# First MoE's last block with five sums of 512 columns at once, and the second product of the block before it behind them

## The chip, the cores and the metric

The kernel runs on one core of one Trainium2 chip. The metric is the device time of one execution in microseconds (us); before the change it was 1115.1 us, the median of three runs (1113.62 to 1118.73).

## What is computed

Three stages follow each other on 1792 tokens (4 batches of 448):

```python
x = attention(q, k, v, g_q, g_k)            # 48 heads of 448 x 64, q and k with an RMS norm
h = x @ moe_w_in                            # first MoE: 1792 x 768 by 768 x 1024
solu = h * softmax(h)
ln = (solu - mean(solu)) / sqrt(var(solu) + 1e-06) * moe_g_ln
x2 = ln @ moe_w_out                         # 1024 x 768
h2 = x2 @ moe2_w_in                         # second MoE: 768 x 2048
out = (h2 - tanh(h2)) @ moe2_w_out          # 2048 x 768
```

The weights arrive as 64-bit numbers and are converted to 32 bits on the chip.

## The kernel before, in words

**Precision.** Each product of the two MoEs is made of three matmuls (`three`, lines 181 to 184): both factors are kept as a high and a low part in fp32r, and high by high, high by low and low by high are added up in PSUM. `split` (lines 186 to 188) makes the parts: ScalarE copies the high one (L187), VectorE subtracts it (L188).

**Blocks.** The first MoE goes over the tokens in four blocks of 384, 384, 384 and 640 tokens; the last is made of a part of 384 and a part of 256, the latter with tiles of its own (`xs+`, `hb+`, `lnT+`) in SBUF space that the attention gives back. A block has these steps: `x_split` loads x from DRAM (`xr`, L496) and splits it into `xs`; `moe_h` computes h (`hps`, TensorE) and copies it to `hb` (L529); `layer_norm` works on `hb` (L545 to L568); `moe_lnT` transposes the result (`lps`, L581) and splits it into `lnT`; `moe_x2` multiplies with `w_out` (`x2ps`) and writes x2 to DRAM (`x2d`, L596).

**Stages.** `stage(b)` holds the work of block b up to its layer norm and the transposes and second product of block b-1. Of the six output chunks d of `moe_x2(b-1)`, the first `XB[b]` stand ahead of `moe_h(b)` and the others behind it. `XB` is 2 for stage 3, the last block's, and 0 for the others. Stages 0 to 2 are interleaved with the attention of batches 1 to 3; stage 3 and stage 4 (block 3's transposes and second product) come when the attention is over.

**moe_h.** The 1024 columns of h are done in four groups of 256. In a group the tokens go in pairs of 128; each pair fills one PSUM bank (pool `ps_m`, three banks) with its six row chunks of the weights one after the other. The stationary operand is 128 tokens of `xs`, the moving one 256 columns of the weights. For block 3 VectorE also takes the maximum of each filled bank (`mx`, L524) before ScalarE copies it.

**Weights.** The converted weights of the first MoE are saved in DRAM in pieces of 512 KB and come back by `Stream.conv` (L174) into a pool `w` of five buffers, in the order of a list of items; an `in` item holds 256 rows by 256 columns, high and low. SP issues these loads in its queue, as it does all others of the stage.

**The second MoE's start.** Ahead of stage 3, `w2.conv(6)` calls for six weight pieces of the second MoE (loads of 512 KB on L115, conversion on POOL, VectorE and ScalarE) and `x2_load(0)` loads and splits x2 of its first 256 tokens (L735, `x2s`). The second MoE's first sums, `h2ps`, take their banks from pool `ps_h`, five banks that the attention held before.

**The order on each engine** is not the order of the code: a planner puts the instructions in the order of its own time model, earlier code first among what is ready in it, and an engine then runs its queue strictly in that order. So work that stands later in the code can come earlier in a queue, where it found a gap.

Of the kernel before, what the change touches and what calls it, by code (L numbers as in the profile page):

```python
# [8 lines left out]
F32 = mybir.dt.float32  # L9
F32R = mybir.dt.float32r  # L10
I32 = mybir.dt.int32
AF = mybir.ActivationFunctionType
ALU = mybir.AluOpType
AX = mybir.AxisListType
# [4 lines left out]
def kernel(  # L19
# [14 lines left out]
    nc = tc.nc  # L34
    B, H, S, D = q.shape
    NTOK, DM = out.shape
    F1 = moe_w_out.shape[0]
# [12 lines left out]
    blocks = [[(0, 384, "")], [(384, 384, "")], [(768, 384, "")], [(1152, 384, ""), (1536, 256, "+")]]  # L50
    NBK = len(blocks)

    XB = [0, 0, 0, 2, 0]

    NQ = 3
    needs = [-(-(b[-1][0] + b[-1][1]) // S) - 1 for b in blocks]
# [25 lines left out]
    def source(kind, i):  # L82
        if kind == "out":
            d, half = divmod(i, 2)
            src = moe_w_out[512 * half:512 * half + 512, 256 * d:256 * d + 256]
            return src.rearrange("(c p) (f z) -> p c f z", p=128, z=2), (4, 128)
        r, c = divmod(i, 3)
        if kind == "out2":
            src = moe2_w_out[256 * r:256 * r + 256, 512 * c:512 * c + 512]
        else:  # L90
            src = (moe_w_in if kind == "in" else moe2_w_in)[256 * c:256 * c + 256, 512 * r:512 * r + 512]
        return src.rearrange("(c p) (f z) -> p c f z", p=128, z=2), (2, 256)

    saved = {}

    class Stream:
# [70 lines left out]
        def conv(self, n):  # L167
            while self.nc < min(n, len(self.items)):
                self.load(self.nc + 1)
                kind, i, again = self.items[self.nc]  # L170
                if again:
                    a, b = source(kind, i)[1]
                    w = self.pool(kind, i).tile([128, 2, a, b], F32R, tag="w6", name="w6")
                    nc.sync.dma_start(out=w.bitcast(F32), in_=saved[kind, i])  # L174
                else:
                    w = self.convert(kind, i, self.pool(kind, i), self.save)
                self.got[self.nc] = self.wide if kind == "out2" else w
                self.nc += 1
                self.load(self.nc + 2)
# [307 lines left out]
    Bp = {}  # L487
    xs_b, hb_t, ln_g, mx_t = {}, {}, {}, {}

    def x_split(b):  # L490
        xs_b[b] = []
        for t0, T, z in blocks[b]:
            xs = Bp["xs" + z].tile([128, 2, KD, T], F32R, tag="xs", name="xs")
            for j in range(0, KD, 2):
                xr = Bp["xr"].tile([128, 2, T], F32, tag="xr", name="xr")
                nc.sync.dma_start(out=xr, in_=xd[:, j:j + 2, t0:t0 + T])  # L496
                split(xs[:, 0, j:j + 2], xs[:, 1, j:j + 2], xr)
            xs_b[b].append(xs)

    def moe_h(b):  # L500
        w0 = w_at["in", b]
        ws.conv(w0 + 3)
        xs_all = xs_b.pop(b)
        hb_t[b] = []
        if b == NBK - 1:
            mx_t[b] = Bp["small"].tile([128, tokens[b] // 128, F1 // 256], F32, tag="mx", name="mx")
        for t0, T, z in blocks[b]:
            hb_t[b].append([Bp["hb" + z].tile([128, F1], F32, tag="hb", name="hb") for _ in range(T // 128)])
        for qq in range(F1 // 256):
            for (t0, T, _), xs, hb in zip(blocks[b], xs_all, hb_t[b]):  # L510
                for tp in range(0, T // 128, 2):
                    n = min(2, T // 128 - tp)
                    ps = ps_m.tile([128, n, 256], F32, tag="m", name="hps")
                    for zi in range(n):
                        cols = slice(128 * (tp + zi), 128 * (tp + zi) + 128)
                        for c in range(KD):
                            w = ws.got[w0 + 3 * qq + c // 2]
                            three(
                                ps[:, zi], (xs[:, 0, c, cols], xs[:, 1, c, cols]),
                                (w[:, 0, c % 2], w[:, 1, c % 2]), c == 0, c == KD - 1,  # L520
                            )
                    if b == NBK - 1:
                        u0 = (t0 - blocks[b][0][0]) // 128 + tp
                        nc.vector.tensor_reduce(  # L524
                            out=mx_t[b][:, u0:u0 + n, qq:qq + 1].rearrange("p u o -> p (u o)"), in_=ps,
                            axis=AX.X, op=ALU.max, negate=True,
                        )
                    for zi in range(n):
                        nc.scalar.activation(  # L529
                            out=hb[tp + zi][:, 256 * qq:256 * qq + 256], in_=ps[:, zi], func=AF.Copy  # L530
                        )
                    if t0 == blocks[b][0][0] and tp == 0:
                        ws.conv(w0 + 3 * qq + 6)
                        if b == 1:
                            for i in range(3 * qq, 3 * qq + 3):
                                ws.convert("out", i, Bp["w"], True)
                    yield n * 1.97

    def layer_norm(b):
        for iu, u in enumerate([u for hb in hb_t[b] for u in hb]):  # L540
# [30 lines left out]
    def moe_lnT(b):  # L571
        ln_g[b] = []
        for (t0, T, y), hb in zip(blocks[b], hb_t.pop(b)):
            G = Bp["lnT" + y].tile([128, 2, KF1, T], F32R, tag="lnT", name="lnT")
            ln_g[b].append(G)
            for t, u in enumerate(hb):
                cols = slice(128 * t, 128 * t + 128)
                for z in range(2):
                    ps = ps_m.tile([128, 4, 128], F32, tag="m", name="lps")
                    for c in range(4):  # L580
                        nc.tensor.transpose(ps[:, c], u[:, 512 * z + 128 * c:512 * z + 128 * c + 128], idf)  # L581
                    split(G[:, 0, 4 * z:4 * z + 4, cols], G[:, 1, 4 * z:4 * z + 4, cols], ps)
                yield 0.9

    def moe_x2(b, d0, d1):
# [13 lines left out]
        if d1 == KD:  # L599
            ln_g.pop(b)  # L600

    def stage(b):

        if b < NBK:
            x_split(b)
        if b > 0:
            yield from moe_lnT(b - 1)
        ln = iter(())
        if b < NBK:
            yield from moe_x2(b - 1, 0, XB[b])  # L610
            yield from moe_h(b)
            ln = layer_norm(b)
            if b == 0:
                for _ in ln:
                    yield 0.5
        if b > 0:
            for cost in moe_x2(b - 1, XB[b], KD):
                next(ln, None)
                yield cost
        for _ in ln:  # L620
            yield 0.5
# [29 lines left out]
    for b in range(NBK + 1):  # L651
        for d in range(KD + 1):
            if d == XB[b] and b < NBK:
                w_at["in", b] = len(items)
                items += [("in", i, b > 0) for i in range(12)]
            if d < KD and b > 0:
                w_at["out", b - 1, d] = len(items)
                items += [("out", i, True) for i in (2 * d, 2 * d + 1)]
# [124 lines left out]
        if sp == NSP - 1 and i < NB - 1:  # L783
            nc.sync.dma_start(out=out[t0:t0 + T, :].rearrange("(t p) d -> p t d", p=128), in_=ob[i])

    w2.conv(6)
    x2_load(0)
    while b <= NBK:
        overlap(b, None)
        b += 1  # L790
# [50 lines left out]
```

## Time and profile before

| | |
|---|---|
| median of three runs | 1115.1 us (1113.62 to 1118.73) |
| profiled execution | 1117.29 us |
| its span, first to last instruction | 1115.4 us |
| TensorE matmuls busy | 1045.5 us, 94% of the span |
| VectorE, ScalarE, POOL busy | 694.8, 493.8 and 234.2 us |
| mean granted TensorE clock | 0.987 of full speed |

The attention ends at about 510 us, stages 3 and 4 lie between 510 and 645 us, the second MoE's main part behind them. A matmul's busy time in the rows is longer than its share of the pipeline: matmuls overlap, and the distance from one start to the next is what TensorE needs for one.

### The profile page before, as it was taken

What the parts mean: (1) busy time and instruction counts of PE and PEld (TensorE: products, weight loads), DVE (VectorE), ACT (ScalarE), POOL (GpSimd) and SP (SyncE); (2) the same over time, 40 slices, a digit from 0 to 9 for tenths busy, and PEclk for the clock granted to TensorE, in tenths of its full rate; (3) what the DMA queues carried; (4) which work ended last, traced back from release to release, by engine and by line L of the source; (5) the groups of instructions that cost most, each with busy time, mean ns of one, the idle gap of its engine ahead of it and who ended that gap; (6) DMA issues with size and microseconds to landing.
All of it is one profiled execution on the core that took longest, in us unless ns stands there. A gap on an engine that the chain in (4) does not pass through costs nothing.

```text
span 1115.4 us, 15528 instructions
## 1 busy us (share of the span) xinstructions
PE 1045.5 (94%) x5528; PEld 874.9 (78%) x5528; DVE 694.8 (62%) x1313; ACT 493.8 (44%) x1004; POOL 234.2 (21%) x204
## 2 busy tenths in 40 slices
PE   4989999988987899998999999999999999999998
PEld 2555666657774778777899989898999989898987
DVE  8776687788797353724655057375767666675444
ACT  4677777777676454744246154321212121212110
POOL 2411123131102000001500025242314241322000
PEclk9999999999998999998999999999999999999999
DMA  7987779957997978655767443121111111120004
GB/s 184 258 230 192 184 213 282 229 167 209 288 285 231 307 207 260 182 174 174 249 205 242 156 152 92 34 65 49 57 38 57 58 58 57 57 57 1 1 29 170
DMA packets 108945, 171.20 MB, mean 153 GB/s; under 512 B 31748, under 2 KB 73156, under 8 KB 108868
## 3 DMA queue, kind: packets, MB, share of 16 engines
q1 hardware_dynamic: 107568, 170.20, 52.2%
q8 instruction: 44, 0.72, 0.3%
q14 instruction: 33, 0.27, 0.1%
q10 hardware_dynamic: 1300, 0.01, 0.1%
HBM read 109.32 MB, written 29.10 MB: 124 GB/s over the span
## 4 chain that ended last, share of the span: by engine, by line
PE 74%; DMA 12%; DVE 7%; ACT 5%; issue 2%; SPq 1%; POOL 0%; ACTq 0%; DVEq 0%; POOLq 0%
PE pvps L401 8%; PE ops L183 7%; PE ops L184 7%; PE ops L182 7%; PE h2ps L183 7%; PE h2ps L184 7%; PE h2ps L182 7%; PE sps L378 4%; PE x2ps L182 3%; PE x2ps L183 3%; PE x2ps L184 3%; PE hps L182 2%; PE hps L184 2%; DMA xr<-xd 2%; PE hps L183 2%; DMA q<-wq 2%
## 5 line engine op out<-in xcount | busy, mean ns | idle before, releaser
L780 DVE TENSOR_TENSOR ob<-ops,ob 128x384 f32<-128x384 f32 x196 | 108.6, 555 | 103.0 <-PE ops L184 102.4
L161 POOL TENSOR_TENSOR w<-val,w 128x512 fp32r<-128x512 f32 x60 | 81.3, 1356 | 419.7 <-ACT w L160 402.6
L401 PE MATMUL pvps<-pf,va 128*128 128x448 f32 (+1 forms) x384 | 160.9, 583 | 1.7 <-ACT pf L387 1.7
L183 PE MATMUL ops<-w,gT 128*128 128x384 f32 x448 | 150.7, 336 | 0.0
L182 PE MATMUL ops<-w,gT 128*128 128x384 f32 x448 | 150.6, 336 | 0.0
L184 PE MATMUL ops<-w,gT 128*128 128x384 f32 x448 | 150.5, 336 | 0.0
L343 DVE TENSOR_REDUCE nm<-mps 128x1 f32<-128x448 f32 x168 | 102.9, 620 | 66.3 <-PE mps L342 57.6
L183 PE MATMUL h2ps<-x2s,w 128*128 128x512 f32 (+1 forms) x384 | 141.0, 367 | 0.0
L184 PE MATMUL h2ps<-x2s,w 128*128 128x512 f32 (+1 forms) x384 | 140.9, 367 | 0.0
L182 PE MATMUL h2ps<-x2s,w 128*128 128x512 f32 (+1 forms) x384 | 140.6, 367 | 0.0
L378 PE MATMUL sps<-q,k 128*128 128x448 f32 (+1 forms) x368 | 117.5, 413 | 20.7 <-ACT pf L387 9.2
L757 ACT ACTIVATE th<-h2ps 128x512 f32<-128x512 f32 (+1 forms) x64 | 34.8, 544 | 181.2 <-PE h2ps L184 180.9
L378 PEld LDWEIGHTS sps<-q,k 128*128 128x128 f32 (+1 forms) x368 | 63.0, 186 | 55.5 <-ACT pf L387 17.8
L387 ACT ACTIVATE pf<-sps 128x448 f32<-128x448 f32 x167 | 88.3, 539 | 37.9 <-PE sps L378 29.5
L182 PE MATMUL hps<-w,xs 128*128 128x256 f32 x336 | 101.0, 301 | 2.7 <-DMA w<-w_in 2.5
L184 PE MATMUL hps<-w,xs 128*128 128x256 f32 x336 | 96.5, 288 | 0.0
L183 PE MATMUL hps<-w,xs 128*128 128x256 f32 x336 | 95.6, 285 | 0.0
L401 PEld LDWEIGHTS pvps<-pf,va 128*128 128x128 f32 (+1 forms) x384 | 61.6, 195 | 42.1 <-issue 34.3
L342 PE MATMUL mps<-k,q 128*128 128x448 f32 (+1 forms) x144 | 77.2, 545 | 14.9 <-DVE nm L343 5.6
L258 POOL TENSOR_TENSOR qn<-qk,rr 112x512 f32<-112x512 f32 x44 | 47.5, 1101 | 192.5 <-DVE rr L239 88.9
L183 PEld LDWEIGHTS ops<-w,gT 128*128 128x128 f32 x448 | 84.3, 188 | 4.6
L182 PEld LDWEIGHTS ops<-w,gT 128*128 128x128 f32 x448 | 84.2, 188 | 4.6 <-DVE ob L780 0.2
(117 smaller groups left out, 2091.7 us busy)
## 6 DMA issues: line engine op xcount, KB each, us to landing
w<-w_out SPq DMA_DIRECT2D x48, 512.0 KB
raw<-in_moe_w_in_dram SPq DMA_DIRECT2D x36, 512.0 KB
raw<-in_moe_w_out_dram SPq DMA_DIRECT2D x36, 512.0 KB
w<-w_in SPq DMA_DIRECT2D x36, 512.0 KB
k<-wk SPq DMA_DIRECT2D x46, 224.0 KB
q<-wq SPq DMA_DIRECT2D x46, 224.0 KB
w_in<-w SPq DMA_DIRECT2D x12, 512.0 KB
w_out<-w SPq DMA_DIRECT2D x12, 512.0 KB
```

The source lines that it names most:

```text
L161: nc.gpsimd.tensor_tensor(out=w[:, 1], in0=x, in1=w[:, 0].bitcast(F32), op=ALU.subtract)
L182: nc.tensor.matmul(ps, lhsT=a[0], rhs=w[0], start=first, stop=False)
L183: nc.tensor.matmul(ps, lhsT=a[0], rhs=w[1], start=False, stop=False)
L184: nc.tensor.matmul(ps, lhsT=a[1], rhs=w[0], start=False, stop=last)
L258: eng.tensor_tensor(out=qn[:, a].rearrange("p c h d -> p h c d"), in0=t[:, a], in1=rr[:, a].rearrange("p h (c o) -> p h c o", o=1).to_broa ...
L342: nc.tensor.matmul(ps, lhsT=qh[:, f:f + 128], rhs=kh, start=True, stop=True)
L343: nc.vector.tensor_reduce(out=nm_t[p][:, c:c + 1], in_=ps, axis=AX.X, op=ALU.max, negate=True)
L378: nc.tensor.matmul(o, lhsT=K[p % NQ][:, i, z, k0:k0 + m], rhs=qcols(Q[p % NQ], slice(0, 128), p, i, z), start=(z == 0), stop=(z == 1))
L387: nc.scalar.activation(out=x, in_=ps, func=AF.Exp)
L401: nc.tensor.matmul(pv_t[n], lhsT=w, rhs=pc_t.pop((n, j))[r], start=first, stop=last)
L757: nc.scalar.activation(out=th, in_=ps, func=AF.Tanh)
L780: nc.vector.tensor_tensor(out=o, in0=ps, in1=o, op=ALU.add)
```

## The change

- `XB[3]` goes from 2 to 0: all six chunks of `moe_x2(2)` stand behind `moe_h` of the last block. The list of weight items follows: twelve items of `w_in` first, then twelve of `w_out`.
- The last block has a function of its own, `moe_h_last`: columns in two groups of 512; five PSUM tiles of 128x512 from pool `ps_h`, one for each 128 tokens; the six row chunks of the weights as the outer loop and the five tiles as the inner one. The maximum and the copy of a tile follow its last row chunk.
- Its weight items (`in1`) hold 128 rows by 512 columns. They are put together from the saved pieces by two DMAs of 256 KB each, with runs of 1 KB in place of 4 KB.
- `x_split(3)` loads row chunks 0 to 3 of both parts ahead of `moe_lnT(2)`, and chunks 4 and 5 behind it.
- `w2.conv(6)` and `x2_load(0)` move from ahead of stage 3 to behind `moe_lnT(2)` and the last `x_split`.

```diff
-    XB = [0, 0, 0, 2, 0]
+    XB = [0, 0, 0, 0, 0]
...
-                    nc.sync.dma_start(out=w.bitcast(F32), in_=saved[kind, i])
+                    if kind == "in1":
+
+                        r, c = divmod(i, 6)
+                        for g in range(2):
+                            nc.sync.dma_start(
+                                out=w[:, :, g].bitcast(F32), in_=saved["in", 3 * (2 * r + g) + c // 2][:, :, c % 2]
+                            )
+                    else:
+                        nc.sync.dma_start(out=w.bitcast(F32), in_=saved[kind, i])
...
-    def x_split(b):
+    def x_split(b, js=range(0, KD, 2)):
...
+        for j in js:
+            for (t0, T, z), xs in zip(blocks[b], xs_b[b]):
                 xr = Bp["xr"].tile([128, 2, T], F32, tag="xr", name="xr")
...
+    def moe_h_last(b):
...
+        for r in range(F1 // 512):
+            ps = [ps_h.tile([128, 512], F32, tag="h", name="hps") for _ in at_]
+            for c in range(KD):
+                ws.conv(w0 + KD * r + c + 4)
+                w = ws.got[w0 + KD * r + c].rearrange("p z g f -> p z (g f)")
+                for u, (xs, cols, hb) in enumerate(at_):
+                    three(
+                        ps[u], (xs[:, 0, c, cols], xs[:, 1, c, cols]), (w[:, 0], w[:, 1]), c == 0, c == KD - 1
+                    )
+                    if c == KD - 1:
+                        nc.vector.tensor_reduce(
+                            out=mx_t[b][:, u, r:r + 1], in_=ps[u], axis=AX.X, op=ALU.max, negate=True
+                        )
+                        copy(nc.scalar, out=hb[:, 512 * r:512 * r + 512], in_=ps[u])
+                yield nt * 0.68
...
+    def second_first():
+
+        w2.conv(6)
+        x2_load(0)
+
     def stage(b):
 
-        if b < NBK:
+        last = b == NBK - 1
+        if last:
+
+            x_split(b, (0, 2))
+        elif b < NBK:
             x_split(b)
         if b > 0:
             yield from moe_lnT(b - 1)
+        if last:
+            x_split(b, (4,))
+            second_first()
         ln = iter(())
         if b < NBK:
             yield from moe_x2(b - 1, 0, XB[b])
-            yield from moe_h(b)
+            yield from (moe_h_last if last else moe_h)(b)
...
-            items += [("in", i, b > 0) for i in range(12)]
+            items += [("in1" if b == NBK - 1 else "in", i, b > 0) for i in range(12)]
...
-    w2.conv(6)
-    x2_load(0)
     while b <= NBK:
```

## Rows read from the trace of the kernel before

**Rows 1.** The page: the span, then DMA share and GB/s in 40 slices.

```profile
span 1115.4 us, 15528 instructions
DMA  7987779957997978655767443121111111120004
GB/s 184 258 230 192 184 213 282 229 167 209 288 285 231 307 207 260 182 174 174 249 205 242 156 152 92 34 65 49 57 38 57 58 58 57 57 57 1 1 29 170
```

**Rows 2.** Windows: stretch, length, busy us (x instructions) of each engine, clock, DMA.

```profile
510.00:520.00 10.00, 5.23 (x27) 4.01 (x25) 7.02 (x11) 7.63 (x14) 1.80 (x2) 0.79 0.22 79
520.00:530.00 10.00, 10.00 (x56) 10.00 (x55) 6.18 (x10) 2.62 (x5) 3.71 (x3) 0.87 0.62 192
530.00:540.00 10.00, 7.96 (x67) 7.75 (x66) 4.44 (x7) 2.35 (x6) 4.08 (x3) 1.00 0.83 282
...
640.00:700.00 60.00, 60.00 (x326) 54.77 (x325) 35.84 (x48) 28.93 (x52) 22.48 (x14) 1.00 0.37 120
```

**Rows 3.** Waits of PE, 500 to 660 us: total us, times, longest.

```profile
PE hps L182 <- DMA w<-w_in: 2.5, 2, 2.0
```

**Rows 4.** Timeline of PE around the transposes of block 2.

```profile
509.29 1.47 PE L581 MATMUL lps<-idf,hb 128*128 128x128 f32 x12
514.07 1.87 PE L581 MATMUL lps<-idf,hb 128*128 128x128 f32 x12 [3.30 <-DVE lnT L188]
516.98 0.66 PE L182 MATMUL x2ps<-lnT,w 128*128 128x384 f32 x1 [1.04 <-ACT lnT L187]
518.55 0.52 PE L184 MATMUL x2ps<-lnT,w 128*128 128x384 f32 x1
...
522.66 0.34 PE L184 MATMUL x2ps<-lnT,w 128*128 128x384 f32 x1
```

**Rows 5.** Timeline of ScalarE and VectorE in the same stretch.

```profile
510.71 1.57 ACT L187 ACTIVATE x2s<-x 128x768 fp32r<-128x768 f32 x2
511.58 1.83 DVE L188 TENSOR_TENSOR x2s<-x,x2s 128x768 fp32r<-128x768 f32 x2 [13.22 <-ACT x2s L187]
512.31 0.60 ACT L187 ACTIVATE lnT<-lps 128x512 fp32r<-128x512 f32 x1
```

**Rows 6.** Timeline of PE: starts in streams of 256 and of 512 columns.

```profile
537.11 0.28 PE L184 MATMUL hps<-w,xs 128*128 128x256 f32 x1
...
544.21 0.28 PE L184 MATMUL hps<-w,xs 128*128 128x256 f32 x1
...
668.96 0.39 PE L182 MATMUL h2ps<-x2s,w 128*128 128x512 f32 x1
...
673.15 0.33 PE L182 MATMUL ops<-w,gT 128*128 128x384 f32 x1
```

**Rows 7.** Windows of tile x2ps alone, behind the last block's h.

```profile
578.20:595.40 17.20, 17.01 (x96) 16.65 (x96) 1.45 (x3) 1.00 0.92 299
```

**Rows 8.** Timeline: end of the layer norm on ScalarE, transposes of block 3 on PE.

```profile
591.99 3.51 ACT L568 ACTIVATE hb<-hb,rs 128x1024 f32<-128x1024 f32 x3
595.42 1.04 PE L581 MATMUL lps<-idf,hb 128*128 128x128 f32 x8
...
602.56 0.45 PE L182 MATMUL x2ps<-lnT,w 128*128 128x384 f32 x1 [0.22 <-DVE lnT L188]
```

**Rows 9.** Timeline of SP's queue: x of the last block.

```profile
476.47 0.37 SPq L496 DMA_DIRECT2D xr<-xd  x1
...
517.44 0.32 SPq L432 DMA_DIRECT2D xd<-xo  x1
520.85 0.88 SPq L496 DMA_DIRECT2D xr<-xd  x2
```

**Rows 10.** Timeline: VectorE and ScalarE read a filled bank of h.

```profile
538.74 0.69 DVE L524 TENSOR_REDUCE mx<-hps 128x2 f32<-128x512 f32 x1
539.46 0.66 ACT L529 ACTIVATE hb<-hps 128x256 f32<-128x256 f32 x2 [6.10 <-DVE mx L524]
```

**Rows 11.** Waits in SP's queue, 480 to 660 us.

```profile
SPq L115 <- DVE val L147: 21.9, 7, 8.5
```

More of the change, by code (lines that the diff above doesn't have):

```diff
@@ L171, in conv @@
                 if again:
-                    a, b = source(kind, i)[1]
+                    a, b = (2, 256) if kind == "in1" else source(kind, i)[1]
                     w = self.pool(kind, i).tile([128, 2, a, b], F32R, tag="w6", name="w6")
-                    nc.sync.dma_start(out=w.bitcast(F32), in_=saved[kind, i])
+                    if kind == "in1":
[6 more added lines that the diff above has]
+                        nc.sync.dma_start(out=w.bitcast(F32), in_=saved[kind, i])
                 else:
@@ L488 @@
     xs_b, hb_t, ln_g, mx_t = {}, {}, {}, {}
-    def x_split(b):
[L491 to L494, printed above, removed]
+    def x_split(b, js=range(0, KD, 2)):
+        if b not in xs_b:
+            xs_b[b] = [Bp["xs" + z].tile([128, 2, KD, T], F32R, tag="xs", name="xs") for _, T, z in blocks[b]]
+        for j in js:
+            for (t0, T, z), xs in zip(blocks[b], xs_b[b]):
                 xr = Bp["xr"].tile([128, 2, T], F32, tag="xr", name="xr")
@@ L497, in x_split @@
                 split(xs[:, 0, j:j + 2], xs[:, 1, j:j + 2], xr)
-            xs_b[b].append(xs)
     def moe_h(b):
@@ L504, in moe_h @@
         hb_t[b] = []
-        if b == NBK - 1:
-            mx_t[b] = Bp["small"].tile([128, tokens[b] // 128, F1 // 256], F32, tag="mx", name="mx")
         for t0, T, z in blocks[b]:
@@ L521, in moe_h @@
                             )
[L522 to L527, printed above, removed]
                     for zi in range(n):
@@ L537, in moe_h @@
                     yield n * 1.97
+    def moe_h_last(b):
+        w0 = w_at["in", b]
+        xs_all = xs_b.pop(b)
+        nt = tokens[b] // 128
+        mx_t[b] = Bp["small"].tile([128, nt, F1 // 512], F32, tag="mx", name="mx")
+        hb_t[b] = [
+            [Bp["hb" + z].tile([128, F1], F32, tag="hb", name="hb") for _ in range(T // 128)] for _, T, z in blocks[b]
+        ]
+        at_ = [
+            (xs, slice(128 * t, 128 * t + 128), hb[t])
+            for (_, T, _), xs, hb in zip(blocks[b], xs_all, hb_t[b]) for t in range(T // 128)
+        ]
+        for r in range(F1 // 512):
[13 more added lines that the diff above has]
+                yield nt * 0.68
     def layer_norm(b):
```

## The prediction

> **What bounds the kernel now.** I read the windows first. From 640 us on TensorE is busy in the whole of every stretch at full clock [rows 2], so nothing done for the other engines there is worth time, and what TensorE gains before 640 us carries through to the end. Between 510 and 540 us it is not so: 5.23 of 10 us busy, then a clock of 0.79 and 0.87, then 7.96 of 10 us [rows 2]. The timeline shows why. TensorE does twelve transposes of block 2's layer norm, waits 3.30 us for VectorE's split of the first, goes on at a lower clock, waits 1.04 us more, and runs its first x2ps matmuls at a distance of 4.11/13 = 0.316 us from start to start (518.55 to 522.66) [rows 4]; 96 of them at full clock took 17.01 us, 0.177 each [rows 7]. The splits were late because ScalarE and VectorE first did the splits of the second MoE's x2, 1.57 and 1.83 us [rows 5]. Then the last block's h waits 2.5 us in all for its weights [rows 3]. The third loss is the transposes of block 3: 40 of them from 595.42 to 602.56 us [rows 8].
>
> **The change, part by part.** The sum is made against the profiled execution: span 1115.4 us [rows 1], 1117.3 us with what lies around it, 2.2 us over the median of 1115.1; I carry the gain over to the median.
>
> *A. The gap at 510 us.* From the end of the first twelve transposes (509.29 + 1.47 = 510.76) to 522.66 us, 11.9 us, TensorE did 12 transposes (1.47/12 = 0.12 each) and 15 x2ps matmuls, 1.5 + 15 x 0.177 = 4.2 us of work at full clock [rows 4, 7]. Lost: 7.7 us. Before the change nothing else could fill it: x2ps needs the transposes, h used the same three banks as they do. After it, h has banks of its own, and I think its matmuls are put into the gap. What they need is there: chunks 0 and 1 of the 384 tokens are loaded long before, and chunks 2 and 3 at 476.47 [rows 9]; the 256 tokens' chunks 0 to 3 are now called for ahead of the transposes and need only the attention's space; the weights of `w_in` come first in the list now, so they fill the five buffers in which two x2 chunks' weights stood. Chunks 4 and 5 hang on the attention's last write, issued at 517.44, after which the load goes out at 520.85 [rows 9]. Twenty tiles' worth of h, chunks 0 to 3, last 20 x 3 x 0.233 = 14.0 us [rows 6], so they carry from 510.8 past 524 us; the load and split of chunks 4 and 5 should end about there. `x2_load(0)`'s splits go behind the transposes', which frees 1.6 us of ScalarE at the start [rows 5]. Bounds: from 1.6 us (only that) to 7.7; I take 7.0, nearer the upper end, since each need is met by a row.
>
> *B. The wait for weights*, 2.5 us [rows 3], goes: it came from `w_in` queued behind four x2 pieces. With five buffers of 128 rows, a buffer is used for 5 x 3 x 0.233 = 3.5 us and has four of these, 14.0 us, from its release to its next use. Demand: 7 more pieces of `w_in`, 3 or 4 of `w_out`, 7 raw pieces of the second MoE, 18 x 0.524 MB in 42 us = 225 GB/s; the slices at nine tenths or more carried 229 to 307 GB/s [rows 1], and 530 to 540 us 282 at 0.83 [rows 2]. Runs of 1 KB in place of 4 KB cost something that no row here separates; between nothing and a rate at the low end (229), it still fits. The 12 additional issues, at 0.37 us each for a load of that queue [rows 9], are 4.4 us of SP in 42 us.
>
> *C. 512 columns.* 60 matmuls of 256 columns lie between the starts 537.11 and 544.21, 0.118 us each; 18 of 512 between 668.96 and 673.15, 0.233 each [rows 6]. 360 x 0.1183 = 42.6 us becomes 180 x 0.2328 = 41.9: 0.7 us gained. Halving the weight loads is worth no more.
>
> The Trainium skill, "TensorE: Matmul & The Clock Gate", section "Back-to-back issue gap", gives about 131 ns for a sustained matmul of 512 columns. By it the 180 would take 23.6 us; the kernel's own 512-column stream at 0.233 us speaks against it, and the sum uses the row.
>
> *D. Changing columns.* All five banks of `ps_h` are full when the first 512 columns end. A bank's next use comes four tiles, 2.8 us, after its last matmul; VectorE needs 0.69 us for the maximum and ScalarE comes after it, not beside it (0.66 us for two halves) [rows 10], so 1.4 us if both are free. A conversion in front on VectorE, or two, makes it late. It is bare, as the second MoE's matmuls want the same banks. Bounds 0 to 3 us; I take 1.0 lost.
>
> *E. x2 of block 2 behind h.* The layer norm of block 3 ended at 591.99 + 3.51 = 595.5, just as the transposes began [rows 8]: four x2 chunks were just enough cover. Six are 6 x 24 x 0.177 = 25.5 us in place of 17, so it is no longer late. The 40 transposes took 7.1 us where 40 x 0.12 = 4.9 would do; they pace with the splits. Second-MoE matmuls that used to slip into h can no longer do so (its banks are taken) and are left for this gap. But `lnT` has one buffer and still waits for block 2's last x2 matmul. Bounds 0 to 2.2 us gained; I take half, 1.1. Weights of x2: 12 pieces in 25.5 us, of which five are in the buffers or on their way, so 7 x 0.524 MB and six x2 writes of 0.2 MB, 190 GB/s, under the 299 of that stretch before [rows 7].
>
> *F. Moved behind the transposes:* the second MoE's six conversions and `x2_load(0)` have until about 640 us; nothing waits for them earlier.
>
> Sum: 7.0 + 2.5 + 0.7 - 1.0 + 1.1 = 10.3 us. 1117.3 becomes 1107.0; in terms of the median, 1115.1 - 10.3 = **1104.8 us**. With nothing lost in A, D and E it is 13.1: 1102.
>
> **The rivals.**
>
> *R1: h does not fill the gap.* The planner puts its matmuls behind the transposes, since by its own times they are ready later, or the 256 tokens' split stands behind the attention's last work. The change then does not do what its reordering promises: A gives 1.6 in place of 7.0, the sum is 4.9, **1110.2 us**. For it: earlier code goes first. Against: the gap is long, and its cause, the three banks, is known to the planner.
>
> *R2: bare waits.* h is without any filler for 42 us, where each of three suppliers can be late: x chunks 4 and 5, the banks at the change of columns, a weight piece. At 2 to 3 us each, 7 us, the sum is 3.3: **1111.8 us**.
>
> *R3: slower.* The weights' loads share SP's queue with the raw loads, which wait for VectorE's conversions, 21.9 us in 7 waits, the longest 8.5 [rows 11]. One such wait and a landing like the 3.4 us of the attention's write [rows 9] are 11.9 us, under the 14.0 of lead. Two in one lead, which now holds twice as many loads of SP, are 17 + 3.4 = 20.4: TensorE stands for 6.4 us. The clock falls after a wait like the one of 3.30 us, where 4.3 us of waits cost 7.7 [rows 4], so the price is 6.4 x 1.8 = 11.5 us. It decides from 10.6 us of blocking on. Once eats the gain; twice gives 1115.1 - 10.3 + 23 = **1127.8 us**. Against: the raw loads also feed nothing urgent, and the queue's order has the early weights in front.
>
> Beside it, the Trainium skill, "DMA: Bandwidth & Descriptors", section "Measured (HBM→SBUF, 128 partitions, SWDGE, issued from GpSimd)", asks for loads of 1 MiB or more; the change halves 512 KB to 256 KB. No run yet shows what that costs here.
>
> *R4: a matmul costs its issue, not its columns.* If the 0.118 us of the 256-column form were the price of a matmul with its weight load, 512 columns would cost the same, 180 x 0.1183 = 21.3 us: C gives 21.3 in place of 0.7, **1084.2 us**. The h2ps stream [rows 6] is the same form on the same engine at 0.233. The page's 131 ns named under C is this rival's nearest support.
>
> **How the numbers follow.** My forecast 0.60, R1 0.20, R2 0.12, R3 0.07, R4 0.01. Half a percent, 5.6 us, is about what a measurement of this kernel can tell from no change; under 1109.5 lie nearly all of the forecast, a third of R1 and R4: 0.65. Within it the rest of R1, R2 and a little of the forecast: 0.27. Slower 0.08, which is R3 and worse cases of R2. The range goes from 1101.5 (all losses gone) to 1113.0, which takes in R1 and most of R2 and leaves out some 0.15.
>
> **What would show it.** A: hps matmuls of 512 columns among or right behind the first lps, no wait of 3 us near 511 and a clock of 1.00 from 510 to 530 us. B: no wait of hps for weights over 1 us. C: starts 0.233 us apart. D: a single pause of hps after its 90th matmul, under 3 us. E: lps of block 3 in under 6 us. The last x2ps of block 3 about 10 us earlier in the span. If hps start only after the last lps at about 516 us, with a low clock, R1 holds; if hps have several pauses, R2; if these name weights and are over 5 us, R3. After 640 us TensorE must stay full; if it does not, the gain is given back there.

## The result and the profile after

The changed kernel takes 1108.4 us (median of 13 runs, 1103.6 to 1114.1) against 1118.7 us for the kernel before on the same chips (13 runs, 1113.6 to 1125.9). The ratio is 0.9903, 95% interval 0.9880 to 0.9926: about 10.8 us or 1.0% gained, where 10.3 were forecast, and clear of the half percent that a measurement can't tell from no change. That the time is 1108.4 and not the 1104.8 of the forecast comes from the starting point: the 13 runs of before lie 3.6 us over the three from which the forecast started. The profiled execution of after took 1109.27 us, with a span of 1107.5 us.

The windows of the changed kernel (columns as in [rows 2]) answer to those of before:

```profile
510.00:520.00 10.00, 10.00 (x46) 7.05 (x46) 4.21 (x7) 6.86 (x12) 0.00 (x0) 1.00 0.55 183
520.00:530.00 10.00, 10.00 (x51) 8.29 (x50) 4.70 (x7) 4.10 (x7) 5.52 (x4) 1.00 0.73 240
530.00:540.00 10.00, 10.00 (x44) 8.09 (x44) 8.46 (x15) 3.63 (x6) 4.66 (x4) 1.00 0.67 209
560.00:570.00 10.00, 9.25 (x54) 8.94 (x53) 9.96 (x26) 6.71 (x13) 0.00 (x0) 1.00 0.76 270
570.00:580.00 10.00, 9.21 (x53) 8.89 (x52) 9.51 (x39) 7.05 (x10) 2.75 (x5) 1.00 0.93 311
640.00:700.00 60.00, 60.00 (x316) 54.41 (x315) 36.19 (x49) 29.69 (x53) 21.48 (x14) 1.00 0.36 116
```

From 510 to 540 us, where TensorE had been busy 5.23, 10.00 and 7.96 of 10 us at clocks of 0.79, 0.87 and 1.00 [rows 2], it is now busy throughout at 1.00. A new hole is 50 us further on, 9.25 and 9.21. After 640 us it is full, as before. The waits of TensorE from 500 to 660 us (total us, times, longest), to be set against [rows 3, 4]:

```profile
PE x2ps L190 <- DMA w<-w_out: 1.5, 2, 0.8
PE lps L609 <- DVE lnT L196: 0.6, 2, 0.3
PE x2ps L190 <- DVE lnT L196: 0.3, 1, 0.3
```

The wait for `w_in` is gone, and the 3.30 us at the transposes too; for them stands a wait for `w_out`, which the kernel before did not have. The timeline of TensorE shows what fills the old gap (L190 to L192 are `three` here, L609 the transposes):

```profile
513.49 1.47 PE L609 MATMUL lps<-idf,hb 128*128 128x128 f32 x12
514.94 0.50 PE L190 MATMUL hps<-w,xs 128*128 128x512 f32 x1
...
522.48 0.40 PE L192 MATMUL hps<-w,xs 128*128 128x512 f32 x1
522.71 1.47 PE L609 MATMUL lps<-idf,hb 128*128 128x128 f32 x12
523.94 0.47 PE L190 MATMUL hps<-w,xs 128*128 128x512 f32 x1
524.26 0.39 PE L191 MATMUL hps<-w,xs 128*128 128x512 f32 x1
...
557.87 0.39 PE L192 MATMUL hps<-w,xs 128*128 128x512 f32 x1
558.10 0.34 PE L190 MATMUL x2ps<-lnT,w 128*128 128x384 f32 x1
```

Between the two halves of the transposes stand 33 matmuls of the last block's h, behind the second half the other 147, without a pause until x2 of block 2 begins.

I read three lengths in every trace. The *stage* runs from the first `lps` of block 2 to the first `h2ps` of 512 columns, that is, to the end of x2; the *tail* from there to the end of the span; what lies before is the attention. The start of the tail in the kernel before and after:

```profile
644.82 0.40 PE L182 MATMUL h2ps<-x2s,w 128*128 128x512 f32 x1
```

```profile
637.93 0.39 PE L190 MATMUL h2ps<-x2s,w 128*128 128x512 f32 x1
```

| us | first `lps` | stage | tail | span |
|---|---|---|---|---|
| before | 509.29 | 135.5 | 470.6 | 1115.4 |
| before, another execution | 506.41 | 137.7 | 470.7 | 1114.8 |
| after | 513.49 | 124.4 | 469.6 | 1107.5 |
| after, another execution | 512.15 | 122.3 | 469.6 | 1104.0 |

So the stage gives 11 to 15 us, more than the whole gain. In the first pair the spans differ by 7.9 us: 11.1 from the stage and 1.0 from the tail, less 4.2 by which the attention ended later. That was not forecast; how much of it belongs to the change is taken up below.

### The profile page after: what moved, and what is told of

The parts are those of the page before. It is cut to its first block, busy times and chain, and to the rows that moved or that the text cites. A ratio compares the mean times of both kernels' runs of the same rounds, so it can differ in the third digit from the quotient of the medians.

```text
span 1107.5 us, 15169 instructions
## 1 busy us (share of the span) xinstructions
PE 1043.3 (94%) x5348; PEld 864.2 (78%) x5348; DVE 690.5 (62%) x1311; ACT 493.1 (45%) x994; POOL 236.4 (21%) x204
## 4 chain that ended last, share of the span: by engine, by line
PE 72%; DMA 15%; DVE 6%; ACT 4%; issue 1%; SPq 1%; POOL 1%; ACTq 0%; DVEq 0%; POOLq 0%
PE pvps L409 9%; PE ops L191 7%; PE ops L192 7%; PE ops L190 7%; PE h2ps L191 7%; PE h2ps L192 7%; PE h2ps L190 7%; PE sps L386 4%; DMA raw<-in_moe_w_out_dram 3%; PE x2ps L190 3%; PE x2ps L191 3%; PE x2ps L192 3%; DMA q<-nt 2%; DMA raw<-in_moe_w_in_dram 2%; DMA w<-w_in 2%; PE mps L350 1%
## 5 line engine op out<-in xcount | busy, mean ns | idle before, releaser
L409 PE MATMUL pvps<-pf,va 128*128 128x448 f32 (+1 forms) x384 | 164.9, 598 | 0.9 <-ACT pf L395 0.9
L190 PE MATMUL ops<-w,gT 128*128 128x384 f32 x448 | 150.3, 336 | 0.0
L192 PE MATMUL ops<-w,gT 128*128 128x384 f32 x448 | 150.2, 335 | 0.0
L192 PE MATMUL h2ps<-x2s,w 128*128 128x512 f32 (+1 forms) x384 | 140.9, 367 | 0.0
L190 PE MATMUL h2ps<-x2s,w 128*128 128x512 f32 (+1 forms) x384 | 140.5, 366 | 0.0
L190 PE MATMUL hps<-w,xs 128*128 128x256 f32 (+1 forms) x276 | 90.6, 329 | 2.6 <-DMA w<-w_in 2.6
L350 PE MATMUL mps<-k,q 128*128 128x448 f32 (+1 forms) x144 | 78.4, 553 | 11.1 <-ACT pf L395 3.3
L190 PEld LDWEIGHTS ops<-w,gT 128*128 128x128 f32 x448 | 84.2, 188 | 4.4
L192 PE MATMUL hps<-w,xs 128*128 128x256 f32 (+1 forms) x276 | 85.9, 313 | 0.0
L191 PE MATMUL hps<-w,xs 128*128 128x256 f32 (+1 forms) x276 | 85.7, 311 | 0.0
```

Source lines behind the costliest of these rows:

```text
L190: nc.tensor.matmul(ps, lhsT=a[0], rhs=w[0], start=first, stop=False)
L191: nc.tensor.matmul(ps, lhsT=a[0], rhs=w[1], start=False, stop=False)
L192: nc.tensor.matmul(ps, lhsT=a[1], rhs=w[0], start=False, stop=last)
L350: nc.tensor.matmul(ps, lhsT=qh[:, f:f + 128], rhs=kh, start=True, stop=True)
L409: nc.tensor.matmul(pv_t[n], lhsT=w, rhs=pc_t.pop((n, j))[r], start=first, stop=last)
```

## The experiments

The ratio is always to the kernel before on the same chip; a difference of 0.001 is 1.1 us. In the diffs, lines marked - are those of the changed kernel unless I say otherwise.

### The order alone, in the kernel before

```diff
-    XB = [0, 0, 0, 2, 0]
+    XB = [0, 0, 0, 0, 0]
```

> The kernel before with XB[3] = 0 and nothing else: block 2's x2 wholly behind h, h still in pairs of 256 columns in the three banks of the transposes, x loaded in the old order. My theory (the gain needs h's own banks and its early x; the order alone takes the cover of 48 x2ps matmuls, 8.4 us, away from the load of x chunks 4 and 5): h cannot enter the gap at 511 us, then runs dry until about 526 to 530 us and waits there for x; the layer norm's cover and the weights' wait give some 3 us back. Time within 4 us of the kernel before, ratio 0.997 to 1.005, TensorE idle twice or more between 510 and 532 us. Rival (the order itself pays): 8 us or more faster, ratio under 0.994.

Measured: 1114.9 us, 0.9975 [0.9949, 1.0001]. The wait of 3.3 us at the transposes stays, the clock is 0.92 and 0.91 in the windows from 510 to 530 us, and TensorE still waits 1.4 us for `w_in`; the stage takes 133.4 us. The long wait for x that I expected is one of 0.5 us.

```profile
PE lps L581 <- DVE lnT L188: 4.3, 4, 3.3
```

The order alone is not the gain.

### The change without the new order

```diff
-    XB = [0, 0, 0, 0, 0]
+    XB = [0, 0, 0, 2, 0]
```

> The changed kernel with XB[3] = 2 again: two chunks of block 2's x2 ahead of h, everything else changed. My theory: one weight piece of w_in is then in the five buffers, enough for 15 matmuls of 512 columns, 3.5 us, in the gap of the transposes, so most of that gap stays filled; what is lost is part of the second gap and some cover of the layer norm: 1 to 4 us slower than the changed kernel, ratio to the kernel before 0.991 to 0.994. Rival (the order itself pays): near the kernel before, ratio 0.997 or more.

Measured: 1115.7 us, 0.9967 [0.9934, 0.9999]; the stage takes 131.4 us. More was lost than I expected. The waits of TensorE:

```profile
PE hps L190 <- DMA w<-w_in: 4.6, 2, 2.8
PE hps L190 <- ACT hb L75: 2.0, 1, 2.0
```

The waits of 1.85 and 2.78 us start at 516 and 523 us, inside the old gap. With two x2 chunks ahead of h their weights stand in the five buffers, and only one piece of `w_in` has been called for when h could begin. TensorE waits for it, fills the gap in part and then stands for weights again, at a clock of 0.84 from 520 to 530 us. What the order brings is that five pieces of `w_in` have been called for by 514 us. The order alone gave 2.8 us and the rest alone 3.7, both intervals reaching to about 1; together they give 10.8.

### The last block's x in the old order

`x_split(3)` loads all chunks of the 384 tokens, then those of the 256, all ahead of the transposes.

```diff
-        for j in js:
-            for (t0, T, z), xs in zip(blocks[b], xs_b[b]):
+        for (t0, T, z), xs in zip(blocks[b], xs_b[b]):
+            for j in js:
...
-            x_split(b, (0, 2))
+            x_split(b)
...
-            x_split(b, (4,))
```

> The changed kernel with the last block's x loaded in the old order: all three pairs of chunks of the 384 tokens first, then those of the 256 tokens, all ahead of the transposes. TensorE's order is the same as in the changed kernel. My theory (early x of the 256 tokens is what lets h into the gap): the load of chunks 4 and 5 of the 384 tokens waits for the attention's last write and holds the 256 tokens' loads behind it, so the fourth tile of the first row chunk waits about 10 us: 7 to 11 us slower than the changed kernel, ratio 0.997 to 1.001. Rival (the banks alone suffice): ratio 0.988 to 0.993.

Measured: 1111.1 us, 0.9945 [0.9914, 0.9977], so 4.7 us of the gain are lost, less than I expected; the stage takes 131.0 us. The planner puts other h matmuls into the gap, those of the 384 tokens, and TensorE waits later:

```profile
PE hps L190 <- ACT hb L75: 2.7, 1, 2.7
PE hps L190 <- ACT xs L195: 2.5, 1, 2.5
```

The 2.7 us are the change of columns, which the forecast priced at 1.0. The timeline of VectorE shows why: a conversion that had itself waited 6.41 us for POOL stands in front of the first maximum.

```profile
535.69 1.75 DVE L139 SCALAR_TENSOR_TENSOR val<-raw,val 128x512 f32<-128x512 f32 x1 [6.41 <-POOL val L138]
537.36 0.68 DVE L561 TENSOR_REDUCE mx<-hps 128x1 f32<-128x512 f32 x1
```

The attention, however, is shorter here than in the changed kernel (below), so the stage's loss of 7 us shows as 4.7 in the time.

### Block 2's transposes in the banks of h

```diff
-                    ps = ps_m.tile([128, 4, 128], F32, tag="m", name="lps")
+                    ps = (ps_h.tile([128, 4, 128], F32, tag="h", name="lps") if b == NBK - 2 else ps_m.tile([128, 4, 128], F32, tag="m", name="lps"))
```

> The changed kernel with block 2's transposes in the five banks of h's sums, so that h's matmuls can't start before the splits have emptied them; all else as changed. My theory (the gap at 510 us, filled with h, is 7 of the 11 us): TensorE stands about 3 us after the first five half tiles, the clock is low for some us behind it, and 5 to 8 us of the gain go: ratio 0.995 to 0.998. Rival (the gain comes from the weights, from 512 columns or from the order): as fast as the changed kernel, ratio 0.988 to 0.993.

Measured: 1110.2 us, 0.9928 [0.9903, 0.9954]. My theory, that separate banks are what the gain hangs on, falls: about 2.8 us are lost, and the interval overlaps that of the changed kernel. TensorE waits 1.3 us for a bank that the attention still held and 1.0 us for a split:

```profile
514.01 2.40 PE L609 MATMUL lps<-idf,hb 128*128 128x128 f32 x20 [1.28 <-ACT xu L427]
517.43 0.66 PE L609 MATMUL lps<-idf,hb 128*128 128x128 f32 x4 [1.01 <-DVE lnT L196]
518.03 0.50 PE L190 MATMUL hps<-w,xs 128*128 128x512 f32 x1
```

No matmul of h stands among the transposes here. With five banks in place of three, twenty of the 24 run in one go, and the gap hardly opens. The clock stays at 1.00, and the stage takes 124.6 us, as in the changed kernel (the wait of 1.3 us lies ahead of it). Five shared banks with an order that lets h follow do nearly what eight do.

### h held behind the transposes

Five added matmuls, whose sums are overwritten at once, tie each bank of h to the last split of block 2's transposes. All else is the changed kernel.

```diff
             ps = [ps_h.tile([128, 512], F32, tag="h", name="hps") for _ in at_]
+            if r == 0:
+                G = ln_g[b - 1][0]
+                for t in ps:
+                    nc.tensor.matmul(
+                        t[:, :256], lhsT=G[:, 1, KF1 - 1, 256:384], rhs=G[:, 1, KF1 - 1, 0:256], start=True, stop=True
+                    )
```

> The changed kernel with five added matmuls of 256 columns (0.6 us) ahead of h's sums, one in each of its banks, that read the last split of block 2's transposes; h overwrites what they leave. The transposes keep their three banks, h keeps its own, but can't start before the last split. My theory, sharpened by the run with shared banks, where the transposes had five banks and stood for only 1.3 and 1.0 us: the price of the gap is the 3.3 us wait at three banks, 1 to 2 us more for the last splits, and the low clock that follows a wait of that length: 6 to 9 us slower than the changed kernel, ratio 0.995 to 0.9985. Rival (filling the gap is worth no more than the 3 us which the shared banks cost): ratio 0.991 to 0.994.

Measured: 1115.7 us, 0.9976 [0.9950, 1.0003]: 8.2 us lost, as the theory had it. The gap is back, in its waits, in the window and in the pace of the first matmuls of h:

```profile
PE lps L615 <- DVE lnT L196: 3.9, 3, 3.3
PE hps L556 <- DVE lnT L196: 2.1, 1, 2.1
```

```profile
510.00:520.00 10.00, 4.93 (x20) 4.14 (x21) 7.02 (x11) 6.57 (x12) 2.90 (x3) 0.68 0.18 56
```

```profile
518.79 0.63 PE L190 MATMUL hps<-w,xs 128*128 128x512 f32 x1
519.22 0.63 PE L191 MATMUL hps<-w,xs 128*128 128x512 f32 x1
```

The stage takes 132.3 us, 7.9 more than in the changed kernel. The five added matmuls are 1.2 us of it, and 1.2 us are a wait at the change of columns. Where the transposes have three banks, the filling of the gap is the main part of the gain.

### Five sums of 256 columns

Four groups of 256 columns, with the old pieces of 512 KB; five tiles from `ps_h` as before.

```diff
-        for r in range(F1 // 512):
-            ps = [ps_h.tile([128, 512], F32, tag="h", name="hps") for _ in at_]
+        for r in range(F1 // 256):
+            ps = [ps_h.tile([128, 256], F32, tag="h", name="hps") for _ in at_]
...
-            items += [("in1" if b == NBK - 1 else "in", i, b > 0) for i in range(12)]
+            items += [("in", i, b > 0) for i in range(12)]
```

> The changed kernel with h's five sums in four groups of 256 columns and the old weight pieces of 256 rows by 256 columns, each one load of 512 KB in runs of 4 KB. My theory: the matmuls cost 0.7 us more, and each of three changes of columns leaves four tiles of 0.36 us, 1.4 us, for maximum (0.42) and copy (0.38) of five tiles that VectorE has to do among conversions, so 1 to 2 us of waiting at each: 2 to 6 us slower than the changed kernel, ratio 0.992 to 0.996. Rival A (512 columns are worth only their 0.7 us): ratio 0.990 to 0.992, waits none. Rival B (the loads of 256 KB in 1 KB runs hold the changed kernel back): faster than it, ratio under 0.988.

Measured: 1119.8 us, 1.0006 [0.9976, 1.0035]: all of the gain is lost, more than I expected, and from another cause. TensorE waits for x, then for `w_in`; the clock is 0.72 in the window of the first wait:

```profile
PE hps L190 <- ACT xs L195: 3.6, 1, 3.6
PE hps L190 <- DMA w<-w_in: 1.3, 1, 1.3
```

```profile
520.00:530.00 10.00, 6.35 (x35) 6.00 (x34) 7.09 (x12) 3.56 (x7) 5.48 (x4) 0.72 0.45 141
```

Chunks 0 to 3 of x last 60 matmuls. At 0.232 us each these are 13.9 us, at 0.118 us 7.1. The first high part of chunks 4 and 5 is ready 14 to 16 us after the first transposes begin in both kernels: in the changed kernel at about 529.3 us, when h reaches chunk 4 at 530.3; here h stands at 521.6 us and waits until 525.2. The width is worth little by its pace and much by its lead. The stage is 8.0 us longer, the tail 1.0. The changes of columns, of which I expected the loss, cost 0.3 us. The rival, that loads of 256 KB hold the changed kernel back, falls as well: with 512 KB loads TensorE waits more for `w_in`.

### The second MoE's start called for early again

```diff
-            second_first()
...
+    second_first()
     while b <= NBK:
```

> The changed kernel with the second MoE's first conversions and x2_load(0) ahead of the last block's stage again. In the changed kernel's trace ScalarE still does the splits of x2_load(0) first, at 514.91 us, ahead of the transposes' splits, so the move did not do what I thought. Theory: same as the changed kernel within 0.25%, ratio 0.988 to 0.993. Rival (the move matters through VectorE's and SP's queues): 3 us or more slower, ratio 0.993 or more.

Measured: 1107.4 us, 0.9888 [0.9848, 0.9927], the same as the changed kernel, with the same order of matmuls up to the end of block 2's x2 and a stage of 123.8 us. Where `w2.conv(6)` and `x2_load(0)` stand in the code is worth nothing that can be measured.

### The raw loads on POOL's queue

The first `w_out` wait of the changed kernel points to SP. In the waits of SP's queue from 545 to 590 us, and its timeline:

```profile
SPq L115 <- DVE val L147: 12.3, 3, 5.4
```

```profile
563.71 0.38 SPq L115 DMA_DIRECT2D raw<-in_moe_w_out_dram  x1
564.18 0.89 SPq L182 DMA_DIRECT2D w<-w_out  x2
```

SP stands for 5.4 us at a raw load whose buffer VectorE has not yet converted (VectorE is 9.96 of 10 us busy here, with the maxima and the layer norm), and two `w_out` loads stand behind it. TensorE has to wait for one of them at 569 us:

```profile
569.42 0.45 PE L190 MATMUL x2ps<-lnT,w 128*128 128x384 f32 x1 [0.75 <-DMA w<-w_out]
```

So the raw loads were moved away from SP:

```diff
-                nc.sync.dma_start(out=t, in_=src)
+                (nc.gpsimd if kind in ("in2", "out2") else nc.sync).dma_start(out=t, in_=src)
```

> The changed kernel with the second MoE's raw weights loaded from POOL's queue instead of SP's. In the changed kernel x2ps waits 0.75 and 0.79 us for w_out, and SP stood 5.4 us at a raw load that waited for VectorE's conversion, with two loads of w_out behind it. Theory (the queue): the two waits go and 1 to 2 us are gained, ratio 0.987 to 0.990. Rival (the DMA engines are full there, 0.93 of the time at 311 GB/s): the waits stay, same time as the changed kernel. Slower by some us if POOL's issuing gets in the way of its conversions.

Measured: 1112.0 us, 0.9936 [0.9911, 0.9962], no gain; the stage takes 126.3 us. SP now stands elsewhere, and TensorE waits longer (waits of TensorE, then of SP):

```profile
PE x2ps L190 <- DMA w<-w_out: 3.4, 2, 3.1
```

```profile
SPq L624 <- ACT x L75: 17.5, 5, 7.6
```

The write of x2 stands ahead of the weights' loads and waits 7.6 us for ScalarE's copy. I read from this that the loads are late because their queue is held, whoever holds it.

### x2's writes on ScalarE's queue, alone and with the raw loads on POOL's

```diff
-                nc.sync.dma_start(out=x2d[:, d, t0:t0 + T], in_=x2)
+                (nc.scalar if b >= NBK - 2 else nc.sync).dma_start(out=x2d[:, d, t0:t0 + T], in_=x2)
```

> The changed kernel with the x2 writes of blocks 2 and 3 issued from ScalarE's queue, right behind the copy that they wait for; the second MoE's raw loads stay in SP's queue. With the raw loads on POOL the waits for w_out came back behind x2 writes (SP stood 7.6 us for ScalarE's copy), so there are two holders. Theory (SP's queue, two holders): half of the cure; x2ps still waits up to 1 us for w_out behind the raw load, at most 1 us gained over the changed kernel, ratio 0.987 to 0.992, and no wait of more than 1.1 us. Rival (the transfers themselves are slow): waits as in the changed kernel, 1.5 us.

Measured: 1105.2 us, 0.9898 [0.9862, 0.9935]. The waits for `w_out` are gone and the stage takes 122.7 us, but the time can't be told from that of the changed kernel. SP still stands 5.0 us at a raw load there, and no wait of TensorE follows; I had expected one of up to 1 us.

The second kernel has this edit and that of the raw loads:

> The changed kernel with the raw loads of the second MoE on POOL's queue and the x2 writes of blocks 2 and 3 on ScalarE's, so that SP's queue holds nothing but loads of weights there. Theory (SP's queue): x2ps no longer waits for w_out, the stretch from block 2's transposes to the end of block 3's x2 takes 122 to 124 us (124.4 in the changed kernel), 1 to 2 us faster than the changed kernel, ratio 0.986 to 0.990. Rival: w_out is late although nothing holds its issue, ratio 0.990 or more.

Measured: 1108.7 us, 0.9934 [0.9913, 0.9956]. No wait for `w_out`, but TensorE waits elsewhere, and the stage takes 127.0 us:

```profile
PE lps L609 <- ACT x L75: 2.9, 1, 2.9
```

None of these moves beats the changed kernel by more than the intervals.

### Both kernels once more

The code of the kernel before, and that of the changed kernel, each in another execution with a profile.

> The kernel before once more, for its trace: how far does the end of the attention (first transposes at 509.29 us there, at 513.49 in the changed kernel) move from one execution to the next? Theory: the stretch from there to the end of x2 is 135.5 us again within 0.5, and the attention's end moves by some us, so that the 4.2 us are an execution's own. Rival (the change delays the attention by 4 us): its end within 1 us of 509.3 again.

> The changed kernel once more, for its trace, beside the one above. Theory: the stretch takes 124.4 us within 0.7, the attention's end lies some us away from 513.49. Rival: within 1 us of it.

Measured: 1116.6 and 1105.8 us, stages of 137.7 and 122.3 us. I expected the stages to repeat closely; they differ by about 2 us from the first executions. The end of the attention differs by 2.9 us between the two executions of before and by 1.3 between those of after. In the second one of after no wait for `w_out` is left, so that wait of 1.5 us belongs to an execution, not to the change as such; and that it is missing in the two kernels above does not show that their moves took it away. The second one of before waits 3.8 us for `w_in`, not 2.5.

## Why the prediction was right, step by step

**A, the gap**, forecast 7.0 us of 7.7. From 514.96 us, the end of the first transposes, to 558.10 TensorE needed 43.1 us for 180 matmuls and 12 transposes, 41.8 + 1.5 = 43.3 by the row's pace: nothing is lost, 7.7 gained. The kernel with h held behind loses 8.2 us again: from its first transposes to its fifth matmul of h lie 12.3 us, 1.2 of them the added matmuls and 3.9 work, so that 7.2 are lost there. The price of the forecast was right. What it needs is stricter than the forecast had it: each of the three preparations (five buffers of `w_in`, x by chunks, 512 columns) loses 4.7 to 11.5 us when it is taken away, though each of these edits takes a little more along (the order of x2, that of h, the weights' pieces). The banks of its own for h, without which the forecast saw nothing to fill the gap, are worth about 2.8: with five banks for the transposes the gap hardly opens, so that it need not be filled.

One statement under A was wrong. `x2_load(0)`'s splits did not go behind the transposes'; ScalarE still does them first, as before [rows 5]:

```profile
514.91 1.58 ACT L195 ACTIVATE x2s<-x 128x768 fp32r<-128x768 f32 x2
516.52 0.60 ACT L195 ACTIVATE lnT<-lps 128x512 fp32r<-128x512 f32 x1
```

It costs nothing, as h covers it. But the lower bound, "from 1.6 us (only that)", rested on code that does not decide the order; the kernel that calls for it early again shows this.

**B, the weights**, forecast 2.5. The waits of h for `w_in` are gone, and 1.5 us came back as waits of x2 for `w_out`, 1.0 net in the profiled execution; in its second execution the changed kernel has neither wait. The step said that demand fits the rate, and it does; what came late was an issue, of the kind that R3 describes. One term of it was too small. A load of a half piece holds SP for 0.60 us in the median (24 instructions of L178, 0.52 to 0.63), not 0.37, so that the new loads take about 10 us more of SP than the old ones and not 4.4; no wait of h came of it.

**C, 512 columns**, forecast 0.7. From 524.26 to 557.87 are 145 steps of 0.232 us, so 180 take 41.8 us against 42.6: 0.8 gained. This is where the Trainium skill, "TensorE: Matmul & The Clock Gate", section "Back-to-back issue gap", had about 131 ns; this trace does not agree with it, and is nearer to the 216 ns that the section gives for an isolated matmul.

**D, the change of columns**, forecast 1.0 lost. No wait names it in the changed kernel. Its bounds of 0 to 3 us hold over the experiments: 0, 0.3, 1.2, 2.0 and 2.7 us. For the 2.7 the trace has a conversion ahead of the first maximum on VectorE; for the others no line here shows the cause.

**E, block 3's transposes**, forecast 1.1. The layer norm now ends 2.8 us before they begin (timelines of ScalarE and of TensorE):

```profile
578.88 3.51 ACT L596 ACTIVATE hb<-hb,rs 128x1024 f32<-128x1024 f32 x3
```

```profile
585.21 1.04 PE L609 MATMUL lps<-idf,hb 128*128 128x128 f32 x8
...
595.72 0.44 PE L190 MATMUL x2ps<-lnT,w 128*128 128x384 f32 x1 [0.28 <-DVE lnT L196]
```

In these 10.5 us stand 36 `h2ps` matmuls of 256 columns, 36 x 0.118 = 4.3 us of work, and 4.9 us of transposes: 1.3 us lost. The 2.2 us that the forecast read as lost before hold three such matmuls, 0.4 us, so that 1.8 were lost and 0.5 is gained. Before, 30 of the 36 were done by 578 us, in the course of h (windows of tile h2ps alone, before and after):

```profile
500.00:578.00 78.00, 4.05 (x30) 3.77 (x30) 0.42 (x1) 0.38 (x1) 0.96 0.61 202
```

```profile
585.00:596.00 11.00, 5.30 (x36) 4.57 (x36) 0.84 (x2) 0.76 (x2) 1.00 0.57 182
```

So the sign that the forecast named, transposes in under 6 us, was not met as it stands: it left out this work, which E itself had moved there.

**Sum.** 7.7 + 1.0 + 0.8 + 0 + 0.5 = 10.0 us for a stage that is 11.1 shorter in this pair. Against the forecast A came out 0.7 us better and D 1.0 better, B 1.5 worse and E 0.6 worse. That the total of the forecast came out so well has in part been luck: these cancel nearly, and so do two more errors, since the stage gives more (13.2 us in the second execution of the changed kernel, 11.7 and 12.8 in the kernels with the early call and with x2's writes moved, each against the first execution of before), and the attention takes some back, as far as the next paragraph can show it.

**What the forecast left out: the attention.** From the 19th of the 24 writes of the attention's result (`xd`) to the first `lps` of block 2 I read 97.6 us in both executions of before, 98.4 in the one with the order alone and 98.0 in the kernel with x in the old order. In the ten executions that have the early loads of the 256 tokens it is 98.6 to 102.2, 100.0 in the mean, and 99.2 and 102.2 in the two executions of the changed kernel. Waits of TensorE for weights from 400 to 505 us stand beside this: none in both executions of before, one of 0.4 us with the order alone; two of 1.4 us in all in the changed kernel, two of 2.8 in its second execution, one of 0.5 with x in the old order.

A candidate stands in SP's queue, before and after:

```profile
438.41 0.77 SPq L496 DMA_DIRECT2D xr<-xd  x1
440.52 0.33 SPq L174 DMA_DIRECT2D w<-w_in  x1
```

```profile
442.70 1.42 SPq L504 DMA_DIRECT2D xr<-xd  x2
444.26 0.37 SPq L182 DMA_DIRECT2D w<-w_in  x1
```

A second load of x is issued there now, ahead of block 2's `w_in`. It does not make that issue late: 7.4 us lie between the 20th write of `xd` and the issue of `w_in` before, and 7.5 after. What could be late is the transfer. One of the two waits fits: in all ten executions with the early load TensorE waits 0.5 to 1.8 us for `w_in` 5 to 7 us behind this issue; in both executions of before and with x in the old order there is no such wait, with the order alone one of 0.4. In the second execution of the changed kernel, the wait and the window behind it:

```profile
446.48 0.38 PE L190 MATMUL hps<-w,xs 128*128 128x256 f32 x1 [1.75 <-DMA w<-w_in]
```

```profile
445.00:450.00 5.00, 3.52 (x10) 1.58 (x10) 0.68 (x1) 1.57 (x3) 0.00 (x0) 0.73 0.92 256
```

There and in the kernel with 256 columns the clock fell to 0.73 and 0.66, and these two have the longest stretches, 102.2 and 101.6 us. The other wait comes 10 us after the 19th write, ahead of the early load, and the kernel with x in the old order has it too; its cause stays open. So the load is argued and not shown: no run moved it alone. And the 19th write itself comes anywhere from 407.9 (h held behind) to 416.2 us (the change without the new order), 408.8 and 411.7 in the two executions of before and 416.0 with the order alone, so that much of the later end of the attention in the first pair lies ahead of the stretch read here and need not belong to the change. If the load is the cause, what the forecast missed stands under A, where the early call of the 256 tokens' x was counted as a need that is met, and its own load was given no price.

**The rivals.** *R1* (h does not fill the gap) did not happen; made to happen, it costs 8.2 us (1.2 of them the added matmuls), against a price of 5.4. *R2* (bare waits in h) did not happen either, but closely: x was there 1 us ahead of its use, and with 256 columns it came 3.6 us late. *R3*: its mechanism is in the trace, a raw load that holds SP 5.4 us with weights behind it; TensorE waited 1.5 us in one execution and not at all in another, far from the 10.6 us of blocking that would decide. Its price of 1.8 us for each us of waiting does not hold everywhere: with the raw loads on POOL's queue a wait of 3.1 us left the clock at 1.00. The forecast put the danger at `w_in`; it hit `w_out`. *R4* (a matmul costs its issue) falls with the 0.232 us.

Beside R3 the forecast named the Trainium skill, "DMA: Bandwidth & Descriptors", section "Measured (HBM→SBUF, 128 partitions, SWDGE, issued from GpSimd)", which asks for loads of 1 MiB or more. The 24 loads of 256 KB made no wait of h here, with 240 GB/s moved from 520 to 530 us; no run shows what larger loads than 512 KB would do.

## What to carry to other kernels

A gap of a matrix engine is filled by work that has space and its inputs at hand: list each of them (accumulators, weights in the buffers, each chunk of the other operand) and see how long the first inputs carry, since a wider inner step carries longer for the same buffers. Ask first whether the gap can be kept from opening, here by two more banks for the transposes. Give a moved load a price where it is issued, also 70 us earlier. And where a planner sets the order, look up where an instruction went before it is given a price.

## What the runs showed of the hardware

- A wait on TensorE costs more than its length where the granted clock falls with it: in the kernel with h held behind, waits of 3.3 and 2.1 us stand in a window with a clock of 0.68, and the first matmuls of h after them start 0.43 us apart, not 0.232. In other kernels waits of 1.0 to 1.3 us left the clock at 1.00 in their windows. The length of one wait does not decide it. For the same weights a wait of 1.75 us stands in a window with a clock of 0.73 (above) and one of 1.80, in the kernel with the raw loads on POOL's queue, in windows with 1.00; and that kernel's wait of 3.1 us for `w_out`, which ends at 577 us, left it at 1.00 too:

```profile
575.00:580.00 5.00, 3.00 (x17) 3.00 (x18) 5.00 (x17) 2.81 (x5) 1.12 (x2) 1.00 0.96 351
```

- The tail is 1.0 us shorter with h of 512 columns (469.5 to 469.9 against 470.6 to 470.7 with 256 columns). None of it is TensorE's: from the first `h2ps` of 512 columns to the last matmul both kernels take 465.8 to 465.9 us. It lies behind the last addition on VectorE (before, then after):

```profile
1111.08 0.56 DVE L780 TENSOR_TENSOR ob<-ops,ob 128x384 f32<-128x384 f32 x1 [0.49 <-PE ops L184]
```

```profile
1104.14 0.56 DVE L820 TENSOR_TENSOR ob<-ops,ob 128x384 f32<-128x384 f32 x1 [0.49 <-PE ops L192]
```

From its start to the end of the span are 4.3 us before and 3.4 after. In the kernel before the last output write ends in slices of 10 to 31 GB/s, which the changed kernel does not have. The cause stays open.
